# Channel-major attention output by small PE tiles, decay factors in PSUM and a second DMA transpose, in a fused recurrent-attention and MLP kernel

## The chip, the cores and the metric

The kernel runs on one core of a Trainium2 chip. The metric is device time in microseconds (us). Several runs of one program are compared by the mean of their fast runs; the profile is one of the runs. A run is called slow when it is over 1.5% above the fastest of the same kernel. The granted TensorE clock (the share of full speed that the matrix engine was given) does not tell such runs apart here: the changed kernel has slow runs at 0.935 and 0.901 and fast ones at 0.946 and 0.931. Medians are of all runs.

## The reference

Inputs have batch B=4, heads H=8, sequence S=768 and head size D=48. The attention is a recurrence over time, one 48x48 state per head. Its output is laid out as 3072 tokens x 384 channels and goes through an MLP with two gates of 1024 channels.

```python
for t in range(S):
    cur = einsum('bhd,bhe->bhde', u * k[t], v[t])
    y[t] = einsum('bhd,bhde->bhe', r[t], state + cur)
    state = w[t][..., None] * state + einsum('bhd,bhe->bhde', k[t], v[t])
x = y.transpose(0, 2, 1, 3).reshape(B * S, H * D)
out = maximum(x @ w1, x @ w2) @ w_out
```

## The kernel before

The sequence is cut into 12 units of 256 tokens of one batch entry. One partition holds two neighbouring tokens (index i). The engines are called PE (matrix products), DVE (VectorE), ACT (ScalarE), POOL or GpSimd, and SP, which here only issues DMAs. In each unit the kernel sums the logarithms of the decay, makes r' = r times the decay and k' = k over the decay, forms scores k'r', masks them, and multiplies by v. The state carried from earlier tokens enters through r'. The maximum of two gates is written as (w1 - w2)x, relu, plus w2 x, so wc = w2 w_out is precomputed. Every operation is a named token, and one list gives the order in which all of them are issued to the engines. All DMAs except the two cast weight loads are issued from one queue, that of SP, strictly in that order. The code is cut to the parts that the change touches.

```python
ORDER = """ ...
k.5 WL.4 Wt.4 evk.4 sc1.4 M1.4 xT.3 g0.3 g1.3 r0.3 r1.3 vd.4 yb.4 sc0.4 M0.4 iA.5 kp.5 ...
oc0.3 oa0.3 ob0.3 oc1.3 os0.3 tr.5 evr.5 kv.5 Sa.5 S1.5 Tf.5 row.5 lp.6 cs.6 AE.6 m.6 AO.6 z.6 ... """

def rp(n): nc.vector.tensor_mul(r_b[n % 2][:, :, :, 0:D], byi(U[n]["r"]), U[n]["A"])      # A in SBUF
def kp(n): nc.vector.tensor_mul(k_b[n % 2][:, :, :, 0:D], byi(U[n]["k"]), U[n]["iA"])     # iA in SBUF

def tr(n):      # r' turned on PE, 8 transposes; evr copies them out of PSUM on ACT
    ...
def evk(n):     # k' turned by the DMA
    nc.sync.dma_start_transpose(out=..., in_=k_b[n % 2].rearrange("s i h d -> s (i h d)"))
def S1(n):      # state cast on DVE, a zero block beside each head
    for e in range(2): nc.vector.tensor_copy(S_1[n % 2][q, :, e * D:(e + 1) * D], U[n]["Sa"][q])

def yb(n): ...  # y[token, channel] : 4 matmuls of 384 columns, then
def yi(n): ...  # 8 of 96 columns (incoming state) and
def ya(n): ...  # 32 of 48 columns (masked scores times v)
def x(n):  nc.scalar.copy(t, U[n]["y"][:, :, 0:HD])
def xT(n): nc.sync.dma_start_transpose(out=..., in_=U[n]["x"]...)   # y turned by the DMA for the MLP

def out_d(n, b):
    for i in range(2):
        nc.sync.dma_start(out=out[tok + i:tok + P:2, :], in_=U[n]["s", b][i * Q:(i + 1) * Q, :])
```

## Time and profile before

| what | value | from |
|---|---|---|
| time | 180.76 us median of 3 (180.09 to 180.93) | runs |
| span of the profile, granted clock | 178.3 us, 0.994 | page |
| busy PE / DVE / ACT / POOL | 135.8 / 126.7 / 91.7 / 106.8 us | page |
| first gate matmul, end of the last PE work | 44.66 us, 173.72 us | timeline of PE |
| gaps of PE in between, the rest | 7.7 us, 121.3 us | summed from that timeline |

From the first gate matmul on, every piece of time in which no matmul is under way is a gap, and what remains is PE work. "L389" and the like are lines of the kernel concerned, so one operation has different numbers in different kernels.

### The profile page before, as it was taken

The numbers are of one execution on the slowest core, as the hardware profiler recorded it, in microseconds if no ns is written. First come the engines' busy times: TensorE is split into PE (matmuls) and PEld (weight loads), VectorE is DVE, ScalarE is ACT, GpSimd is POOL, SyncE is SP. The second block draws the span as 40 slices with busy tenths as digits, with TensorE's granted clock in tenths as the row PEclk, the third lists the DMA queues.
The fourth block names the chain that finished last, engine by engine and source line by source line (L and its number), as shares of the span: only waits on it lengthen the run. The fifth ranks groups of instructions, "written<-read, shape, count | busy, mean of one in ns | idle before, by whom it ended". The sixth has DMA issues, their size and how long they took to land.

```text
span 178.3 us, 4629 instructions
## 1 busy us (share of the span) xinstructions
PE 135.8 (76%) x1912; PEld 87.9 (49%) x1912; DVE 126.7 (71%) x163; ACT 91.7 (51%) x153; POOL 106.8 (60%) x96
## 2 busy tenths in 40 slices
PE   0324064505999987978998889989999999999990
...
DMA  5988799699925979998889879999999988171513
GB/s 146 269 174 162 131 309 315 95 175 249 260 49 120 285 165 161 287 187 228 223 194 263 172 178 248 169 307 164 244 258 189 266 197 240 26 169 26 114 37 74
DMA packets 85445, 33.56 MB, mean 188 GB/s; under 512 B 80424, under 2 KB 84648, under 8 KB 85424
## 3 DMA queue, kind: packets, MB, share of 16 engines
...
## 4 chain that ended last, share of the span: by engine, by line
PE 33%; DMA 24%; DVE 17%; POOL 12%; issue 6%; SPq 4%; ACT 2%; POOLq 0%; ACTq 0%
PE go L456 11%; PE go L480 7%; DVE rn L263 6%; DMA wo_sb<-in_moe_w_out_dram 5%; POOL rku L299 5%; DVE S L360 4%; DMA w_sb<-in_moe_w_dram 4%; DMA xT<-x 4%; PE go L475 3%; DMA u_b<-in_u_dram 3%; DMA out_dram<-osb 3%; PE go L215 3%; DVE kn L267 3%; DMA lw<-in_w_dram 2%; DMA lr<-in_r_dram 2%
## 5 line engine op out<-in xcount | busy, mean ns | idle before, releaser
L456 PE MATMUL go<-xT,wd_sb 128*128 128x256 bf16 x288 | 37.4, 276 | 3.8 <-DMA xT<-x 1.9
L464 ACT ACTIVATE gT<-go 128x512 bf16<-128x512 f32 x48 | 28.5, 596 | 21.0 <-PE go L456 19.8
L393 DVE TENSOR_TENSOR M<-sc,mask 128x1024 bf16<-128x1024 f32 x24 | 29.3, 1219 | 12.8 <-PE sc L389 12.7
L480 PE MATMUL go<-wo_sb,gT 128*128 128x384 bf16 x192 | 35.3, 326 | 0.0
L294 POOL TENSOR_TENSOR rku<-lr,lk 128x768 f32<-128x768 f32 x12 | 21.8, 1814 | 20.2 <-issue 10.5
L456 PEld LDWEIGHTS <-wd_sb 128*128 128x128 bf16 x288 | 26.9, 99 | 10.5 <-issue 4.9
L299 POOL TENSOR_TENSOR rku<-rku,u_b 128x768 f32<-128x768 f32 x12 | 28.2, 2350 | 0.4 <-DMA u_b<-in_u_dram 0.3
L480 PEld LDWEIGHTS <-gT 128*128 128x128 bf16 x192 | 18.6, 98 | 14.1 <-issue 1.8
L263 DVE TENSOR_TENSOR rn<-lr,A 128x768 bf16<-128x768 f32 x12 | 25.1, 2095 | 0.1
L310 POOL TENSOR_TENSOR vd<-lv,dg 128x768 bf16<-128x768 f32 x12 | 17.7, 1475 | 11.2 <-DVE dg L305 10.7
L231 POOL TENSOR_TENSOR lp<-lw 128x384 f32<-128x384 f32 x12 | 17.4, 1447 | 3.1 <-ACT lw L226 3.1
L267 DVE TENSOR_TENSOR kn<-lk,iA 128x768 bf16<-128x768 f32 x12 | 18.6, 1550 | 0.1
L236 PE MATMUL ex<-lp,triS 128*128 128x384 f32 x24 | 13.0, 631 | 7.4 <-POOL lp L231 7.4
L360 DVE CAST S<-Sa 64x192 bf16<-64x192 f32 x24 | 17.6, 734 | 0.6
L485 ACT COPY osb<-go 128x384 f32<-128x384 f32 x24 | 11.3, 472 | 12.1 <-PE go L480 12.1
L389 PE MATMUL sc<-rT,kT 48*64 48x128 bf16 x384 | 10.7, 232 | 8.3 <-DMA kT<-kn 7.0
L326 ACT COPY rT<-tr 128x1024 bf16<-128x1024 bf16 x12 | 12.1, 1010 | 9.0 <-PE tr L319 9.0
L475 PE MATMUL go<-wc_sb,xT 128*128 128x384 bf16 x72 | 15.7, 328 | 0.0
L389 PEld LDWEIGHTS <-kT 48*64 48x64 bf16 x384 | 6.7, 112 | 17.0 <-DMA kT<-kn 8.9
L242 ACT ACTIVATE A<-ex 128x384 f32<-128x384 f32 x12 | 5.9, 490 | 15.5 <-PE ex L236 15.5
L305 DVE TENSOR_REDUCE dg<-rku 128x16 f32<-128x768 f32 x12 | 11.3, 942 | 3.4 <-POOL rku L299 3.4
L442 ACT CAST x<-y 128x768 bf16<-128x768 f32 x12 | 9.5, 791 | 7.9 <-PE y L433 7.8
...
## 6 DMA issues: line engine op xcount, KB each, us to landing
...
```

The source lines that it names most:

```text
L231: nc.gpsimd.tensor_add(t, U[n]["lw"][:, :, 0, :], U[n]["lw"][:, :, 1, :])
L263: nc.vector.tensor_mul(r_b[n % 2][:, :, :, 0:D], byi(U[n]["r"]), U[n]["A"])
L267: nc.vector.tensor_mul(k_b[n % 2][:, :, :, 0:D], byi(U[n]["k"]), U[n]["iA"])
L294: nc.gpsimd.tensor_mul(t, U[n]["r"], U[n]["k"])
L299: nc.gpsimd.tensor_mul(t, t, u_b.rearrange("p (h d) -> p h d", h=H).unsqueeze(1).to_broadcast([P, 2, H, D]))
L310: nc.gpsimd.tensor_mul(t.rearrange("p i h d -> p h i d"), U[n]["v"], U[n]["dg"].to_broadcast([P, H, 2, D]))
L360: nc.vector.tensor_copy(S_1[n % 2][q, :, e * D:(e + 1) * D], U[n]["Sa"][q])
L393: nc.vector.tensor_mul(t.rearrange("s e p t -> s (e p) t"), U[n]["sc", i].rearrange("s e p t -> s (e p) t"), mask[:, i].rearrange("s i q - ...
L456: nc.tensor.matmul(g[:, f, :], wd_sb[:, ko, fo * P:(fo + 1) * P], U[n]["xT"][:, :, ko, :], start=(f == 0 and ko == 0), stop=(f == 1 and ko ...
L464: nc.scalar.activation(U[n]["gT"][:, 2 * j:2 * j + 2].rearrange("p f j t -> p (f j t)"), U[n]["g", j].rearrange("p f j t -> p (f j t)"), A ...
L475: nc.tensor.matmul(t, U[n]["xT"][:, b, ko, :], wc_sb[:, ko, :], start=(ko == 0), stop=False)
L480: nc.tensor.matmul(U[n]["o", b], U[n]["gT"][:, fo, b, :], wo_sb[:, fo, :], start=False, stop=(fo == FO - 1))
```

## The change

It moves work off DVE and PE. The decay factors are computed in place in two PSUM banks. The attention output is produced with channels on the partitions, so it needs no transpose before the MLP. r' is then turned by the DMA, like k'. The state cast goes to ACT as one copy, and the whole order of issue is new, with the weights loaded first. The diff is shortened; its lines without code name what went.

```diff
-    ex, A, iA                               # sum in one PSUM bank, factors in SBUF
+    EX = ps.tile([P, 2, 512], F32, tag="ex", name="ex")      # sum and factors, one buffer, in place
-        nc.vector.tensor_mul(r_b[n % 2][:, :, :, 0:D], byi(U[n]["r"]), U[n]["A"])
+        nc.vector.tensor_mul(r_b[n % 2][:, :, :, 0:D], byi(U[n]["r"]), fac())
-    tr, evr, evk, x, xT(DMA)
+    def turn(n, name, src):
+        U[n][name] = t = wt_([P, 2, NP, P], BF16, name)
+        nc.sync.dma_start_transpose(out=..., in_=src[n % 2].rearrange("s i h d -> s (i h d)"))
+    OP["rT"] = lambda n: turn(n, "rT", r_b)
+    OP["kT"] = lambda n: turn(n, "kT", k_b)
-        for e in range(2): nc.vector.tensor_copy(S_1[...], U[n]["Sa"][q])
+        nc.scalar.copy(U[n]["S1"], U[n]["Sa"])
 ...
+    WIN = ((0, 0), (0, 1), (1, 1), (1, 2))      # head of the pair, 32-channel window
+    # 32 matmuls 48x32, 128 columns (incoming state), 64 matmuls 64x32, 128 columns (scores):
+    nc.tensor.matmul(out32(n, p, w, b), vwin(n, q, i, p, w * 32, 32), U[n]["M", i][q, WIN[w][0], p, :], ...)
+    def xT(n): nc.scalar.copy(t.rearrange("c b k t -> c b (k t)"), U[n]["y"][:, :, 0:HD])
 ...
+v.7 vb.7 vd.7 w.8 lw.8 lp.8 k.8 r.8 rk.8 rku.8 WL.6 out1.3 M0.6 sc1.6 rp.7 iA.7 rT.7 ... oc0.5 oa0.5
+ob0.5 oc1.5 os0.5 M1.6 ya.6 xT.6 out0.5 oa1.5 ob1.5 os1.5 kp.7 kT.7 kv.7 Sa.7 S1.7 cs.8 ... g0.6
+g1.6 r0.6 r1.6 ... yb.7 yi.7 sc0.7 M0.7 row.7 AE.8 g2.6 g3.6 r2.6 r3.6
```

More of the change, by code (lines that the diff above doesn't have):

```diff
@@ L17 @@
 ORDER = """
-w.0 k.0 lw.0 lp.0 cs.0 AE.0 m.0 r.0 u rk.0 rku.0 v.0 w.1 w2 k.1 vb.0 z.0 wt.0 AO.0 rp.0 tr.0
-iA.0 kp.0 kv.0 Sa.0 S1.0 lw.1 lp.1 cs.1 AE.1 m.1 AO.1 z.1 iA.1 dg.0 vd.0 kp.1 evk.0 evr.0 sc0.0
-M0.0 Tf.0 sc1.0 M1.0 yb.0 yi.0 ya.0 x.0 r.1 rp.1 tr.1 rk.1 evr.1 rku.1 dg.1 v.1 w.2 lw.2 vb.1
-kv.1 Sa.1 vd.1 S1.1 Tf.1 yb.1 lp.2 cs.2 AE.2 w1 wo wd.2 wd.0 wd.1 wcm.0 wce.0 xT.0 g0.0 r0.0
-row.0 m.2 AO.2 z.2 evk.1 sc1.1 M1.1 g1.0 r1.0 wt.1 wcm.1 wce.1 WL.0 Wt.0 dec.0 S0.0 wt.2 wcm.2
-wce.2 k.2 sc0.1 M0.1 iA.2 kp.2 g2.0 r2.0 g3.0 r3.0 yi.1 ya.1 x.1 r.2 v.2 rk.2 vb.2 w.3 lw.3 rp.2
@@ L24 @@
-rku.2 dg.2 oc0.0 oa0.0 ob0.0 oc1.0 os0.0 oa1.0 tr.2 evr.2 kv.2 Sa.2 S1.2 Tf.2 ob1.0 os1.0 row.2
-lp.3 cs.3 AE.3 k.3 WL.2 Wt.2 evk.2 sc1.2 M1.2 xT.1 g0.1 g1.1 r0.1 r1.1 row.1 m.3 AO.3 z.3 vd.2
-yb.2 sc0.2 M0.2 iA.3 kp.3 g2.1 r2.1 g3.1 r3.1 r.3 v.3 rk.3 vb.3 w.4 lw.4 rp.3 rku.3 dg.3 yi.2
-ya.2 x.2 WL.1 Wt.1 out0.0 oc0.1 oa0.1 ob0.1 oc1.1 os0.1 tr.3 evr.3 kv.3 Sa.3 S1.3 Tf.3 row.3
-lp.4 cs.4 AE.4 m.4 AO.4 z.4 oa1.1 ob1.1 os1.1 out1.0 k.4 WL.3 Wt.3 dec.1 evk.3 sc1.3 M1.3 xT.2
-g0.2 g1.2 r0.2 r1.2 vd.3 yb.3 sc0.3 M0.3 iA.4 kp.4 g2.2 r2.2 g3.2 r3.2 dec.2 S0.2 r.4 v.4 rk.4
@@ L30 @@
-vb.4 w.5 lw.5 rp.4 rku.4 dg.4 yi.3 ya.3 x.3 oc0.2 oa0.2 ob0.2 oc1.2 os0.2 tr.4 evr.4 kv.4 Sa.4
-S1.4 Tf.4 row.4 lp.5 cs.5 AE.5 m.5 AO.5 z.5 oa1.2 ob1.2 os1.2 out1.1 out0.1 k.5 WL.4 Wt.4 evk.4
-sc1.4 M1.4 xT.3 g0.3 g1.3 r0.3 r1.3 vd.4 yb.4 sc0.4 M0.4 iA.5 kp.5 g2.3 r2.3 g3.3 r3.3 dec.3
-S0.3 r.5 v.5 rk.5 vb.5 w.6 lw.6 rp.5 rku.5 dg.5 yi.4 ya.4 x.4 oc0.3 oa0.3 ob0.3 oc1.3 os0.3 tr.5
-evr.5 kv.5 Sa.5 S1.5 Tf.5 row.5 lp.6 cs.6 AE.6 m.6 AO.6 z.6 out0.2 oa1.3 ob1.3 os1.3 S0.1 out1.2
-k.6 WL.5 Wt.5 evk.5 sc1.5 M1.5 xT.4 g0.4 g1.4 r0.4 r1.4 vd.5 yb.5 sc0.5 M0.5 iA.6 kp.6 g2.4 r2.4
@@ L36 @@
-g3.4 r3.4 dec.4 S0.4 r.6 v.6 rk.6 vb.6 w.7 lw.7 rp.6 rku.6 dg.6 yi.5 ya.5 x.5 oc0.4 oa0.4 ob0.4
-oc1.4 os0.4 tr.6 evr.6 kv.6 Sa.6 S1.6 Tf.6 row.6 lp.7 cs.7 AE.7 m.7 AO.7 z.7 out0.3 oa1.4 ob1.4
-os1.4 out1.3 k.7 WL.6 Wt.6 evk.6 sc1.6 M1.6 xT.5 g0.5 g1.5 r0.5 r1.5 vd.6 yb.6 sc0.6 M0.6 iA.7
-kp.7 g2.5 r2.5 g3.5 r3.5 dec.5 S0.5 r.7 v.7 rk.7 vb.7 w.8 lw.8 rp.7 rku.7 dg.7 yi.6 ya.6 x.6
-oc0.5 oa0.5 ob0.5 oc1.5 os0.5 tr.7 evr.7 kv.7 Sa.7 S1.7 Tf.7 row.7 lp.8 cs.8 AE.8 m.8 AO.8 z.8
-out0.4 oa1.5 ob1.5 os1.5 out1.4 k.8 WL.7 Wt.7 evk.7 sc1.7 M1.7 xT.6 g0.6 g1.6 r0.6 r1.6 vd.7
@@ L42 @@
-yb.7 sc0.7 M0.7 iA.8 kp.8 g2.6 r2.6 g3.6 r3.6 dec.6 S0.6 r.8 v.8 rk.8 vb.8 w.9 lw.9 rp.8 rku.8
-dg.8 yi.7 ya.7 x.7 oc0.6 oa0.6 ob0.6 oc1.6 os0.6 tr.8 evr.8 kv.8 Sa.8 S1.8 lp.9 cs.9 AE.9 m.9
-AO.9 z.9 out0.5 oa1.6 ob1.6 os1.6 out1.5 k.9 evk.8 sc1.8 M1.8 xT.7 g0.7 g1.7 r0.7 r1.7 vd.8 yb.8
-sc0.8 M0.8 iA.9 kp.9 g2.7 r2.7 g3.7 r3.7 dec.7 S0.7 r.9 v.9 rk.9 vb.9 w.10 lw.10 rp.9 rku.9 dg.9
-yi.8 ya.8 x.8 oc0.7 oa0.7 ob0.7 oc1.7 os0.7 tr.9 evr.9 kv.9 Sa.9 S1.9 lp.10 cs.10 AE.10 m.10
-AO.10 z.10 out0.6 oa1.7 ob1.7 os1.7 out1.6 k.10 evk.9 sc1.9 M1.9 xT.8 g0.8 g1.8 r0.8 r1.8 vd.9
@@ L48 @@
-yb.9 sc0.9 M0.9 iA.10 kp.10 g2.8 r2.8 g3.8 r3.8 r.10 v.10 rk.10 vb.10 w.11 lw.11 rp.10 rku.10
-dg.10 yi.9 ya.9 x.9 oc0.8 oa0.8 ob0.8 oc1.8 os0.8 tr.10 evr.10 kv.10 Sa.10 S1.10 lp.11 cs.11
-AE.11 m.11 AO.11 z.11 out0.7 oa1.8 ob1.8 os1.8 out1.7 k.11 evk.10 sc1.10 M1.10 xT.9 g0.9 g1.9
-r0.9 r1.9 vd.10 yb.10 sc0.10 M0.10 iA.11 kp.11 g2.9 r2.9 g3.9 r3.9 r.11 v.11 rk.11 vb.11 rp.11
-rku.11 dg.11 yi.10 ya.10 x.10 oc0.9 oa0.9 ob0.9 oc1.9 os0.9 tr.11 evr.11 kv.11 Sa.11 S1.11
-out0.8 oa1.9 ob1.9 os1.9 out1.8 evk.11 sc1.11 M1.11 xT.10 g0.10 g1.10 r0.10 r1.10 vd.11 yb.11
@@ L54 @@
-sc0.11 M0.11 g2.10 r2.10 g3.10 r3.10 yi.11 ya.11 x.11 oc0.10 oa0.10 ob0.10 oc1.10 os0.10 out0.9
-oa1.10 ob1.10 os1.10 out1.9 xT.11 g0.11 g1.11 r0.11 r1.11 g2.11 r2.11 g3.11 r3.11 oc0.11 oa0.11
-ob0.11 oc1.11 os0.11 out0.10 oa1.11 ob1.11 os1.11 out1.10 out0.11 out1.11
+w.0 w1 lw.0 w2 wt.2 wd.2 k.0 r.0 u v.0 lp.0 cs.0 wo wcm.2 wd.1 m.0 z.0 AO.0 w.1 row.0 wd.0 AE.0
+rp.0 rT.0 iA.0 rk.0 rku.0 dg.0 vd.0 vb.0 lw.1 lp.1 kp.0 kv.0 kT.0 cs.1 Sa.0 S1.0 Tf.0 m.1 z.1
+AO.1 AE.1 yb.0 yi.0 sc1.0 M1.0 sc0.0 wce.2 M0.0 ya.0 k.1 r.1 rp.1 rk.1 rku.1 dg.1 iA.1 kp.1 wt.1
@@ new lines @@
+wcm.1 wce.1 wt.0 wcm.0 wce.0 v.1 vb.1 vd.1 w.2 lw.2 lp.2 k.2 r.2 rk.2 rku.2 xT.0 kv.1 Sa.1 S1.1
+Tf.1 g0.0 g1.0 r0.0 r1.0 cs.2 m.2 z.2 AO.2 AE.2 rT.1 kT.1 yb.1 yi.1 sc0.1 M0.1 row.1 dg.2 g2.0
+r2.0 g3.0 r3.0 WL.0 Wt.0 v.2 vb.2 vd.2 w.3 k.3 lw.3 lp.3 r.3 rk.3 rku.3 sc1.1 WL.1 rp.2 iA.2
+rT.2 row.2 oc0.0 oa0.0 ob0.0 os0.0 out0.0 oc1.0 oa1.0 M1.1 ya.1 xT.1 ob1.0 os1.0 kp.2 kT.2 kv.2
+Sa.2 S1.2 Tf.2 cs.3 m.3 z.3 AO.3 g0.1 r0.1 g1.1 r1.1 yb.2 yi.2 sc0.2 AE.3 WL.2 g2.1 g3.1 r2.1
+r3.1 dg.3 out1.0 M0.2 sc1.2 v.3 vb.3 vd.3 w.4 k.4 lw.4 lp.4 r.4 rk.4 rku.4 row.3 rp.3 iA.3 rT.3
@@ new lines @@
+oc0.1 oa0.1 ob0.1 oc1.1 os0.1 out0.1 M1.2 ya.2 xT.2 oa1.1 ob1.1 os1.1 kp.3 kT.3 kv.3 Sa.3 S1.3
+Tf.3 cs.4 g0.2 g1.2 r0.2 r1.2 WL.3 m.4 z.4 AO.4 AE.4 dec.0 S0.0 yb.3 yi.3 sc0.3 g2.2 g3.2 r2.2
+r3.2 dg.4 M0.3 sc1.3 v.4 vd.4 vb.4 w.5 k.5 lw.5 lp.5 r.5 rk.5 rku.5 Wt.1 rp.4 iA.4 rT.4 row.4
+oc0.2 oa0.2 ob0.2 oc1.2 os0.2 out0.2 M1.3 ya.3 xT.3 dec.1 S0.1 oa1.2 ob1.2 os1.2 out1.1 kp.4
+kT.4 kv.4 Sa.4 S1.4 Tf.4 cs.5 m.5 z.5 AO.5 dg.5 g0.3 g1.3 r0.3 r1.3 WL.4 AE.5 yb.4 yi.4 sc0.4
+M0.4 g2.3 g3.3 r2.3 r3.3 v.5 vb.5 vd.5 w.6 lw.6 lp.6 k.6 r.6 rk.6 rku.6 sc1.4 row.5 rp.5 iA.5
@@ new lines @@
+rT.5 oc0.3 oa0.3 ob0.3 oc1.3 os0.3 out0.3 Wt.2 dec.2 S0.2 WL.5 M1.4 ya.4 xT.4 oa1.3 ob1.3 os1.3
+out1.2 kp.5 kT.5 kv.5 Sa.5 S1.5 Tf.5 cs.6 m.6 z.6 AO.6 g0.4 g1.4 r0.4 r1.4 yb.5 yi.5 sc0.5 AE.6
+dg.6 g2.4 g3.4 r2.4 r3.4 M0.5 sc1.5 v.6 vb.6 vd.6 w.7 lw.7 lp.7 k.7 r.7 rk.7 rku.7 rp.6 iA.6
+rT.6 oc0.4 oa0.4 ob0.4 os0.4 oc1.4 out0.4 M1.5 ya.5 xT.5 oa1.4 ob1.4 os1.4 kp.6 kT.6 kv.6 Sa.6
+S1.6 Tf.6 cs.7 m.7 z.7 AO.7 dg.7 Wt.3 dec.3 S0.3 g0.5 g1.5 r0.5 r1.5 yb.6 yi.6 sc0.6 row.6 AE.7
+g2.5 g3.5 r2.5 r3.5 v.7 vb.7 vd.7 w.8 lw.8 lp.8 k.8 r.8 rk.8 rku.8 WL.6 out1.3 M0.6 sc1.6 rp.7
@@ new lines @@
+iA.7 rT.7 Wt.5 Wt.4 dec.4 S0.4 out1.4 oc0.5 oa0.5 ob0.5 oc1.5 os0.5 M1.6 ya.6 xT.6 out0.5 oa1.5
+ob1.5 os1.5 kp.7 kT.7 kv.7 Sa.7 S1.7 cs.8 Tf.7 m.8 z.8 AO.8 dg.8 g0.6 g1.6 r0.6 r1.6 dec.5 S0.5
+yb.7 yi.7 sc0.7 M0.7 row.7 AE.8 g2.6 g3.6 r2.6 r3.6 v.8 vb.8 vd.8 w.9 lw.9 lp.9 k.9 r.9 rk.9
+rku.9 sc1.7 WL.7 Wt.6 dec.6 S0.6 rp.8 iA.8 rT.8 oc0.6 oa0.6 ob0.6 oc1.6 os0.6 out0.6 M1.7 ya.7
+xT.7 oa1.6 ob1.6 os1.6 kp.8 kT.8 kv.8 Sa.8 S1.8 cs.9 m.9 z.9 AO.9 dg.9 g0.7 g1.7 r0.7 r1.7 yb.8
+yi.8 sc0.8 AE.9 g2.7 g3.7 r2.7 r3.7 M0.8 sc1.8 out1.5 v.9 vb.9 vd.9 w.10 lw.10 lp.10 k.10 r.10
@@ new lines @@
+rk.10 rku.10 rp.9 iA.9 rT.9 oc0.7 oa0.7 ob0.7 os0.7 oc1.7 out0.7 M1.8 ya.8 xT.8 out1.6 oa1.7
+ob1.7 os1.7 kp.9 kT.9 kv.9 Sa.9 S1.9 cs.10 m.10 z.10 AO.10 g0.8 g1.8 r0.8 r1.8 yb.9 yi.9 sc0.9
+AE.10 g2.8 g3.8 r2.8 r3.8 dg.10 M0.9 sc1.9 v.10 vb.10 vd.10 w.11 lw.11 lp.11 k.11 r.11 rk.11
+rku.11 v.11 vb.11 rp.10 iA.10 rT.10 oc0.8 oa0.8 ob0.8 oc1.8 os0.8 out0.8 M1.9 ya.9 xT.9 oa1.8
+ob1.8 os1.8 kp.10 kT.10 kv.10 Sa.10 S1.10 cs.11 m.11 z.11 AO.11 g0.9 g1.9 r0.9 r1.9 out1.8 dg.11
+vd.11 Wt.7 dec.7 S0.7 yb.10 yi.10 sc0.10 AE.11 g2.9 g3.9 r2.9 r3.9 M0.10 sc1.10 rp.11 iA.11
@@ L57 @@
+rT.11 oc0.9 oa0.9 ob0.9 oc1.9 os0.9 M1.10 ya.10 xT.10 oa1.9 ob1.9 os1.9 kp.11 kT.11 kv.11 Sa.11
+S1.11 g0.10 g1.10 r0.10 r1.10 yb.11 yi.11 sc0.11 out0.9 g2.10 g3.10 r2.10 r3.10 M0.11 sc1.11
+oc0.10 oa0.10 ob0.10 oc1.10 out1.7 os0.10 out0.10 out1.9 M1.11 ya.11 xT.11 oa1.10 ob1.10 os1.10
+g0.11 r0.11 g1.11 r1.11 g2.11 g3.11 r2.11 oc0.11 oa0.11 r3.11 ob0.11 oc1.11 os0.11 out0.11
+oa1.11 ob1.11 os1.11 out1.10 out1.11
 """
@@ L91, in _body @@
     DP = 64
+    VW = 80
     NU = NC * B
@@ L124, in _body @@
     mask = const.tile([P, 2, 2, Q], F32)
-    sel = const.tile([P, 2, 2, Q], BF16)
     MZ = [const.tile([P, 2, H, DP], F32, name=f"mz{i}") for i in range(2)]
@@ L132, in _body @@
             nc.vector.memset(t.rearrange("p i h d -> p (i h) d")[:, :, D:DP], 0.0)
-    S_f = [const.tile([P, NP, D], F32, name=f"Sf{b}") for b in range(B)]
-    T_f = [const.tile([P, NP, D], F32, name=f"Tf{b}") for b in range(B)]
-    S_0 = [const.tile([P, NP, 2 * D], BF16, name=f"S0{b}") for b in range(B)]
-    S_1 = [const.tile([P, NP, 2 * D], BF16, name=f"S1{b}") for b in range(2)]
-    nc.vector.memset(sel, 0.0)
+    v_b = [const.tile([P, 2, H, VW], BF16, name=f"vn{i}") for i in range(3)]
+    for t in v_b:
+        nc.gpsimd.memset(t[:, :, ::2, D:VW], 0.0)
+    S_f = [const.tile([P, NP, DP], F32, name=f"Sf{b}") for b in range(B)]
+    T_f = [const.tile([P, NP, DP], F32, name=f"Tf{b}") for b in range(B)]
+    S_0 = [const.tile([P, NP, DP], BF16, name=f"S0{b}") for b in range(B)]
+    EX = ps.tile([P, 2, 512], F32, tag="ex", name="ex")
     for b in range(2):
@@ L142, in _body @@
         for i in range(2):
-            nc.vector.tensor_copy(sel[q, i, i, :], ident[q, q])
             for i2 in range(2):
@@ L146, in _body @@
                                       (triI if (i, i2) == (0, 1) else triS)[q, q])
-    for t in S_f + S_1 + S_0:
+    for t in S_f + S_0:
         nc.vector.memset(t, 0.0)
@@ L234, in cs, with ex3, fac, m @@
     def cs(n):
-        U[n]["ex"] = t = pt_([P, H, D], F32, "ex")
-        nc.tensor.matmul(t.rearrange("p h d -> p (h d)"), triS,
-                         U[n]["lp"].rearrange("p h d -> p (h d)"))
+        nc.tensor.matmul(EX[:, 0, 0:HD], triS, U[n]["lp"].rearrange("p h d -> p (h d)"))
+    def ex3():
+        return EX[:, 0, 0:HD].rearrange("p (h d) -> p h d", h=H)
+    def fac():
+        return EX[:, :, 0:HD].rearrange("p i (h d) -> p i h d", h=H)
+    @op
+    def m(n):
+        nc.vector.tensor_add(MZ[n % 2][:, 0, :, 0:D], ex3(), U[n]["lw"][:, :, 0, :])
+    @op
+    def z(n):
+        nc.vector.tensor_add(MZ[n % 2][:, 1, :, 0:D], ex3(), U[n]["lp"])
+    @op
+    def AO(n):
+        nc.scalar.activation(fac()[:, 1], MZ[n % 2][:, 0, :, 0:D], AF.Exp)
     @op
     def AE(n):
-        U[n]["A"] = t = wt_([P, 2, H, D], F32, "A")
-        nc.scalar.activation(t[:, 0], U[n]["ex"], AF.Exp)
-    @op
-    def m(n):
-        nc.vector.tensor_add(MZ[n % 2][:, 0, :, 0:D], U[n]["ex"], U[n]["lw"][:, :, 0, :])
-    @op
-    def z(n):
-        nc.vector.tensor_add(MZ[n % 2][:, 1, :, 0:D], U[n]["ex"], U[n]["lp"])
-    @op
-    def AO(n):
-        nc.scalar.activation(U[n]["A"][:, 1], MZ[n % 2][:, 0, :, 0:D], AF.Exp)
+        nc.scalar.activation(ex3(), ex3(), AF.Exp)
     @op
     def iA(n):
-        U[n]["iA"] = t = wt_([P, 2, H, D], F32, "iA", 1)
-        nc.scalar.activation(t, MZ[n % 2][:, :, :, 0:D], AF.Exp, scale=-1.0)
+        nc.scalar.activation(fac(), MZ[n % 2][:, :, :, 0:D], AF.Exp, scale=-1.0)
     @op
     def rp(n):
-        nc.vector.tensor_mul(r_b[n % 2][:, :, :, 0:D], byi(U[n]["r"]), U[n]["A"])
+        nc.vector.tensor_mul(r_b[n % 2][:, :, :, 0:D], byi(U[n]["r"]), fac())
     @op
     def kp(n):
-        nc.vector.tensor_mul(k_b[n % 2][:, :, :, 0:D], byi(U[n]["k"]), U[n]["iA"])
+        nc.vector.tensor_mul(k_b[n % 2][:, :, :, 0:D], byi(U[n]["k"]), fac())
     @op
@@ L287, in vb @@
     def vb(n):
-        U[n]["vb"] = t = wt_([P, H, 2, D], BF16, "vb", 3)
-        nc.gpsimd.tensor_copy(t, U[n]["v"])
+        nc.gpsimd.tensor_copy(v_b[n % 3][:, :, :, 0:D], byi(U[n]["v"]))
     @op
@@ L311, in vd @@
                              U[n]["dg"].to_broadcast([P, H, 2, D]))
-    @op
-    def tr(n):
-        U[n]["tr"] = tp = pt_([P, NP, 2, 2, Q], BF16, "tr")
-        for i in range(2):
-            for p in range(NP):
-                nc.tensor.transpose(
-                    tp[:, p, :, i, :],
-                    r_b[n % 2][:, i, 2 * p:2 * p + 2, :].rearrange("s r d -> s (r d)"), ident)
-    @op
-    def evr(n):
-        U[n]["rT"] = t = wt_([P, NP, 2, 2, Q], BF16, "rT")
-        nc.scalar.copy(t, U[n]["tr"])
-    @op
-    def evk(n):
-        U[n]["kT"] = t = wt_([P, 2, NP, P], BF16, "kT")
+    def turn(n, name, src):
+        U[n][name] = t = wt_([P, 2, NP, P], BF16, name)
         nc.sync.dma_start_transpose(out=t.rearrange("d i p q -> d (i p) q"),
-                                    in_=k_b[n % 2].rearrange("s i h d -> s (i h d)"))
+                                    in_=src[n % 2].rearrange("s i h d -> s (i h d)"))
+    OP["rT"] = lambda n: turn(n, "rT", r_b)
+    OP["kT"] = lambda n: turn(n, "kT", k_b)
     @op
```

93 lines of the change are left out of this document (49 added, 44 removed).

## The prediction

> **What bounds the kernel now.** I read the page first, then the chain in order of time, the groups by shape, single lines with the spread of their durations, then the loading of the weights in the timeline of the first 50 us, and the DMA queue's own instructions.
>
> From the page of the kernel before (engine totals, then two rows of the 40 slices of 4.46 us, each digit a tenth busy):
>
> ```profile
> PE 135.8 (76%) x1912; PEld 87.9 (49%) x1912; DVE 126.7 (71%) x163; ACT 91.7 (51%) x153; POOL 106.8 (60%) x96
> PE   0324064505999987978998889989999999999990
> DMA  5988799699925979998889879999999988171513
> ```
>
> PE is busy 0 to 6 tenths in the first ten slices (44.6 us) and 7 to 9 in nearly all later ones. So there are two stages: a start of 44.7 us, in which the weights arrive and attention unit 0 is made, and 128.8 us in which PE works through twelve units (first gate matmul at 44.66 us, last PE work at 173.5). A tail of 4.8 us follows (copy and store of the last rows).
>
> From the chain that ended last, in order of time (start us, us, what), most of one unit:
>
> ```profile
> 139.00 0.81 PE go L456 x6
> 139.81 0.43 PE y L409 x4
> 140.25 0.35 PE sc L389 x16
> 140.60 1.42 PE go L456 x12
> 142.01 0.34 PE y L421 x8
> 142.35 0.51 PE y L433 x32
> 142.86 0.59 PE go L475 x3
> 143.45 1.30 PE go L480 x8
> 144.75 0.49 PE go L475 x3
> 145.24 0.04 issue
> 145.28 0.62 PE tr L319 x8
> 145.90 0.38 PE y L344 x16
> ```
>
> The reader sees the price of each PE step without gaps. One unit: gates 2.9 (24 in 2.93 at the end of the chain), second layer 16 in 2.6, wc product 0.59+0.49, L409 0.43, scores 2 x 0.35, L421 0.34, L433 0.51, transposes 0.62, k'v 0.4, prefix sum 0.9. Sum 10.5 us. The starts of the L409 group in the timeline (59.63 to 160.29 us, nine units) give 11.2 us per unit: 12.2 and 12.1 at first, about 11.1 in the middle, 10.7 to 9.9 at the end. So about 0.7 us of each unit is PE waiting. In the chain these waits are DVE work: r' 2.5 us, k' 1 to 1.3, the state cast 1.3.
>
> From the groups by line (busy us, mean ns; then idle time before):
>
> ```profile
> L263 DVE TENSOR_TENSOR rn<-lr,A 128x768 bf16<-128x768 f32 x12 | 25.1, 2095 | 0.1
> L267 DVE TENSOR_TENSOR kn<-lk,iA 128x768 bf16<-128x768 f32 x12 | 18.6, 1550 | 0.1
> L360 DVE CAST S<-Sa 64x192 bf16<-64x192 f32 x24 | 17.6, 734 | 0.6
> L393 DVE TENSOR_TENSOR M<-sc,mask 128x1024 bf16<-128x1024 f32 x24 | 29.3, 1219 | 12.8 <-PE sc L389 12.7
> ```
>
> Per unit DVE has 2.1 + 1.55 + 2 x 0.73 + 2 x 1.22, and reduce 0.94, two sums 1.1, Sa and Tf 0.7: 10.3 us, as much as PE. The views of single lines (min/median/max ns) tell why the first three are dear:
>
> ```profile
> L263 DVE TENSOR_TENSOR rn<-lr,A x12: 946/2561/2569, 9.6 to 154.7; 128x768 bf16<-128x768 f32 x12
> L393 DVE TENSOR_TENSOR M<-sc,mask x24: 1211/1223/1226, 23.2 to 161.2; 128x1024 bf16<-128x1024 f32 x24
> ```
>
> The same product takes 946 ns or 2,569 ns, while the mask product, with one operand in PSUM, is always 1.21 to 1.23 us.
>
> **What the Trainium skill says.** (1) "SBUF — State Buffer", section Who interferes with whom: a DVE instruction with two SBUF inputs contends with GpSimd reads, and so does a two-port copy or cast; one with at most one SBUF input does not. The trace agrees: r' spreads over 946 to 2,569 ns, the mask product over 15. (2) "TensorEngine Tiling (Array Packing)", Performance Considerations and Restrictions: tiling speeds up TensorE but not PSUM evacuation; column tiling excludes fast weight loads, and different row tiles must not use the same PSUM bank together. The kernel before shows 64-column tiles working at 22 ns a pair; no run yet shows 32-column ones. (3) "TensorE: Matmul & The Clock Gate", Part 3, The mechanism: a weight load overlaps running matmuls only where the row group differs. The trace fits: k'v takes 0.37 us for 32 pairs when its row tile alternates, but 0.38 us for 16 pairs in the last chunk, where it does not (12 against 24 ns).
>
> **The change, part by part.**
>
> *Factors in PSUM.* r' and k' now read one operand from PSUM. I put both at the uncontended 0.95 us: DVE saves 1.15 + 0.6 = 1.75 us per unit, and GpSimd is blocked less (its u product is 1.81 us alone, 2.35 on average). The cost is a serial chain through one buffer: sum 0.9, m and z 1.1, two exponentials 1.0, r' 0.95, inverse 0.84, k' 0.95, some 5.7 us plus handovers. It fits in an 11 us unit.
>
> *State casts.* Two DVE casts (1.47 us) become one 128x256 ACT copy, about 0.4 us by the 0.47 us of the 128x384 copy. GpSimd's two 0.34 us casts become one. DVE falls to some 10.3 - 1.75 - 1.47 + 0.1 = 7.2 us per unit. DVE stops being a bound.
>
> *r' by the DMA.* PE loses 0.62 us (tr) and ACT the 1.01 us copy. The transpose of x disappears, as the output is already channel-major; ACT still copies y (0.79 us). DMA trades 6 blocks for 8 of 128x128. At the end of the trace one pair of transposes (458 KB) holds the DMA share at 0.98 for about 2.5 us, so the trade costs about 0.35 us of DMA. With four loads (at 325 GB/s, seen in windows, 4.8 us), stores 1.8 and both transposes, 9.2 us per unit: below 11. The wait for xT (4.1 us and 2.6 us in two places of the chain) goes; r' and k' each get a DMA wait of 3.5 us, which the new order covers with PE work.
>
> *Channel-major output.* L409 4 x 384 columns (0.43 us) becomes 12 pairs of 64 columns: at L433's 16 ns, 0.2. L421 and L433 (0.85 us, 8 + 32 pairs) become 32 + 64 pairs with 128 moving columns. Scores, also 128 columns in 64-row tiles, take 22 ns a pair. The 64 of L433 alternate row tiles; with twice the column tiles but one column tile visited twice running, I take 18 ns: 1.15 us. The 32 of L421 go two by two on a row tile; 26 ns, between 22 and 24 with a margin: 0.83 us. Together 2.0, so +1.15. PE per unit: 10.5 - 0.62 - 0.23 + 1.15 = **10.8 us**. PE work does not fall; what can fall is its waiting, from 0.7 to an estimated 0.2 us: 11.0 us a unit.
>
> *The start.* Before, w_out is issued only at 32.4 us (behind GpSimd's work of unit 1) and lands at 42.1. Now w1, w2 and w_out go first. w2 took 6.95 us alone; with w and w1 beside it I estimate landing at 14 us, w_out at 22. But k, r, v of unit 0 are issued behind the w2 transpose, so at 15 to 17 us, landing 19 to 22. Then: GpSimd products to 24, reduce to 25, k' to 26, its transpose to 31, scores and masks one after the other to 35, output 36, two weight products and k'v of unit 1 to 40.5. I put the first gate at **40.5 us**, against 44.7, with all three weight products done by then (before, two were still to come, 2.6 us).
>
> *Sum.* From the first gate: 12 x 6.6 us of MLP + 11 x 4.2 of attention = 125.4, less 1.2 for first-chunk units without the incoming state, plus 11 x 0.2 of waits = 126.4. 40.5 + 126.4 + 4.8 = 171.7 us of span; the timed median is 2.5 us over the span (180.76 against 178.3): 174.2, which I round up to **174.5 us**, as the estimates of the start leave out handovers.
>
> **The rivals.** *Small tiles cost more than thought.* If 32-column pairs take 40 ns, L421 and L433 become 3.8 us, PE 12.7 us per unit, and the time some 195 us. For it: without row alternation a pair doubled to 24 ns, and the skill page says fast weight loads are off. Against it: scores already run in column tiles at 22 ns. *The waits vanish and tiles are quick.* At 13 ns a pair PE needs 10.1 us per unit: 166 us. *A transpose arrives late.* k' is transposed behind stores in the queue; DMA_TRANSPOSE takes 1.25 us to issue and 3.2 to 5.1 to land. Half a microsecond per unit gives 180 us. *The start does not shorten* (units' loads behind weights): 178 to 180 us.
>
> **Range and chances.** The start is uncertain by 3 us, PE per unit by 0.4 (5 us in all). Range 167 to 181 us. Faster by over 2% (under 177.1) 0.70; within 2% 0.22; slower 0.08.
>
> **What would show it.** Right: r' and k' at 0.95 us with hardly any spread; DVE busy near 90 us in all; L421 and L433 successors summing to 2 us per unit; first gate near 40 us; w_out landed before 25; units 11 us apart with PE at 9 tenths. Wrong: PE waiting on rT or kT transposes in the middle; a pair cost of 30 ns or more; a first gate at 44 us or later; ACT waits for the prefix sum showing the single factor buffer as the bound.

## The result

The changed kernel is slower: 190.6 us median of four runs (188.34 to 193.59), against 180.84 us for the kernel before in the same rounds. The ratio is 1.040, 95% interval 1.027 to 1.054. A ratio here is the mean time of one kernel's fast runs over the mean of the other's in the same rounds, so it is not quite the ratio of the medians. Two of the four runs count as slow (192.7 and 193.6 us). The profiled run is a fast one, 188.51 us, span 186.6, clock 0.946. The prediction of 174.5 us, range 167 to 181, was wrong.

From the page of the changed kernel: totals, then PE and its granted clock in 40 slices of 4.67 us.

```profile
PE 135.2 (72%) x2536; PEld 85.9 (46%) x2536; DVE 90.8 (49%) x132; ACT 83.3 (45%) x153; POOL 94.1 (50%) x91
PE   0303227777969969829949989699996497999980
PEclk9999999999996999965996999969999999999996
```

DVE fell from 126.7 to 90.8 us of work, as intended. But PE's row, which was 8 to 9 in the middle before, has holes of 2, 4 and 6, and behind some of them the granted clock falls to 6 and 5 tenths.

| from the timeline of PE | before | changed | difference |
|---|---|---|---|
| first gate matmul at | 44.66 | 40.12 | -4.5 |
| gaps of PE after it | 7.7 | 19.7 | +12.0 |
| PE work after it | 121.3 | 121.3 | 0.0 |
| from PE's end to the end of the span | 4.6 | 5.5 | +0.9 |
| span | 178.3 | 186.6 | +8.3 |

So the start was gained as predicted, and twelve microseconds of waiting were added. The waits of the changed kernel (who waited for what: us in total, times, longest) say what for:

```profile
PE sc L379 <- DMA kT<-kn: 17.8, 9, 3.9
ACT lw L227 <- DMA lw<-in_w_dram: 16.8, 8, 3.2
```

Scores wait for the transposed k' in nine of the twelve units, 17.8 of the 19.7 us. After its first gate the kernel before waited 0.93 us for the same thing. The chain that ended last (start us, us, what) and the DMA queue's own instructions in the timeline show one such wait, of unit 5:

```profile
93.66 0.47 DVE mz L250
94.15 3.13 DMA kT<-kn
97.28 0.04 issue
97.32 0.42 PE sc L379 x16
97.74 2.38 PE go L456 x12
```

```profile
88.06 0.95 DVE L270 TENSOR_TENSOR kn<-lk,ex 128x768 bf16<-128x768 f32 x1 [0.26 <-ACT ex L262]
...
90.85 2.01 SPq L281 DMA_DIRECT2D WL<-row  x1
92.91 1.14 SPq L491 DMA_DIRECT2D out_dram<-osb  x2
94.15 1.28 SPq L318 DMA_TRANSPOSE kT<-kn  x1
```

k' was complete at 89.01. Its transpose was issued at 94.15, 5.1 us later, because SP first waited 0.6 us for what the stores needed and then issued four stores and a small reload. The data landed 3.1 us after the issue. Over units 1 to 11 this lag from DVE's end to the issue is 2.0 us on average, and from issue to landing it is 3.1 to 5.0 us in the nine waits. In units 2 to 11 of the kernel before the lag was 0.4 us (unit 1, 9.3 us, belongs to its start).

The last line of the chain above also shows the second loss. Twelve gate matmuls take 2.38 us, where a full clock gives 1.42. A wait of 1.64 us before 55.90 us is followed by this (the view by windows: stretch and its length, busy us and instructions of PE, PEld, DVE, ACT, POOL, then granted clock, DMA share, GB/s):

```profile
55.00:56.00 1.00, 0.10 (x8) 0.10 (x12) 0.42 (x1) 0.47 (x2) 0.00 (x0) 1.00 0.62 71
57.00:58.00 1.00, 1.00 (x7) 0.58 (x5) 1.00 (x2) 0.60 (x1) 0.00 (x0) 0.53 0.56 104
59.00:60.00 1.00, 1.00 (x4) 0.46 (x3) 1.00 (x1) 0.00 (x0) 0.00 (x0) 0.50 1.16 323
61.00:62.00 1.00, 1.00 (x13) 0.43 (x14) 0.00 (x0) 0.71 (x1) 1.00 (x2) 1.00 1.13 297
```

The clock is halved from about 57.1 to 60.5 us and then restored. PE work stayed at 121.3 us although the new matmuls cost less; e5 below puts that down to the clock.

The halvings do not follow from the length of a single gap. They begin at 57.05, 80.95, 98.01 and 121.91 us, whole multiples of 3.41 us apart. Here are two stretches of that grid in which the clock held, and the one before the first halving:

```profile
39.99:43.40 3.41, 2.77 (x61) 1.83 (x45) 1.87 (x4) 1.50 (x3) 2.63 (x3) 1.00 0.92 164
43.40:46.82 3.42, 2.69 (x48) 2.00 (x49) 2.22 (x3) 2.26 (x5) 1.94 (x2) 1.00 0.99 251
53.64:57.05 3.41, 1.77 (x45) 1.33 (x45) 1.63 (x2) 1.83 (x4) 0.79 (x1) 1.00 0.80 148
```

The stretches before the four halvings have PE busy for 1.77, 1.17, 0.95 and 1.42 us. No other full stretch at full clock between the first gate and 180 us has under 1.79. A gap of 1.37 us before 44.13 falls across two stretches and left the clock alone. The limit is not exact: in e6 a stretch with 1.68 us was not followed by a halving. This is read from traces; no experiment moved a gap for it.

### The profile page after: what moved, and what is told of

Read it like the earlier page. It is cut to its first block, busy times and chain, and to the rows that moved or that the text cites. A ratio compares the mean times of both kernels' runs of the same rounds, so it can differ in the third digit from the quotient of the medians.

```text
span 186.6 us, 5852 instructions
## 1 busy us (share of the span) xinstructions
PE 135.2 (72%) x2536; PEld 85.9 (46%) x2536; DVE 90.8 (49%) x132; ACT 83.3 (45%) x153; POOL 94.1 (50%) x91
## 4 chain that ended last, share of the span: by engine, by line
PE 38%; DMA 34%; SPq 9%; POOL 6%; DVE 4%; ACT 4%; issue 3%; POOLq 0%; DVEq 0%; ACTq 0%
DMA kT<-kn 14%; PE go L480 13%; PE go L456 11%; DMA lw<-in_w_dram 9%; PE go L475 6%; DMA lr<-in_r_dram 6%; DMA w_sb<-in_moe_w_dram 5%; PE sc L379 4%; SPq L208 3%; SPq L178 3%; PE y L440 2%; SPq L491 2%; POOL rku L301 2%; POOL rku L296 2%; PE y L333 2%
## 5 line engine op out<-in xcount | busy, mean ns | idle before, releaser
L456 PE MATMUL go<-xT,wd_sb 128*128 128x256 bf16 x288 | 39.6, 292 | 0.1
L296 POOL TENSOR_TENSOR rku<-lr,lk 128x768 f32<-128x768 f32 x12 | 21.7, 1810 | 24.8 <-DMA lr<-in_r_dram 24.8
L456 PEld LDWEIGHTS <-wd_sb 128*128 128x128 bf16 x288 | 28.9, 104 | 9.1 <-issue 2.4
L291 POOL CAST vn<-lv 128x768 bf16<-128x768 f32 x12 | 9.9, 825 | 31.8 <-DMA lv<-in_v_dram 26.1
L379 PE MATMUL sc<-rT,kT 48*64 48x128 bf16 x384 | 11.6, 248 | 19.2 <-DMA kT<-kn 17.8
L301 POOL TENSOR_TENSOR rku<-rku,u_b 128x768 f32<-128x768 f32 x12 | 21.7, 1810 | 0.9
L227 ACT ACTIVATE lw<-lw 128x768 f32<-128x768 f32 x12 | 10.1, 842 | 16.9 <-DMA lw<-in_w_dram 16.8
L270 DVE TENSOR_TENSOR kn<-lk,ex 128x768 bf16<-128x768 f32 x12 | 11.4, 952 | 12.2 <-ACT ex L262 12.2
L475 PE MATMUL go<-wc_sb,xT 128*128 128x384 bf16 x72 | 17.1, 351 | 0.0
L254 ACT ACTIVATE ex<-mz 128x384 f32<-128x384 f32 x12 | 5.9, 494 | 22.5 <-DVE mz L250 21.2
L349 DVE TENSOR_TENSOR Sa<-y,Sf 128x256 f32<-128x256 f32 x12 | 5.1, 424 | 21.9 <-PE y L333 19.2
L232 POOL TENSOR_TENSOR lp<-lw 128x384 f32<-128x384 f32 x12 | 12.0, 998 | 2.8 <-ACT lw L227 2.8
L262 ACT ACTIVATE ex<-mz 128x768 f32<-128x768 f32 x12 | 9.6, 802 | 7.6 <-DVE rn L266 7.5
```

Of the source, the lines that this page charges most:

```text
L232: nc.gpsimd.tensor_add(t, U[n]["lw"][:, :, 0, :], U[n]["lw"][:, :, 1, :])
L296: nc.gpsimd.tensor_mul(t, U[n]["r"], U[n]["k"])
L301: nc.gpsimd.tensor_mul(t, t, u_b.rearrange("p (h d) -> p h d", h=H).unsqueeze(1).to_broadcast([P, 2, H, D]))
L379: nc.tensor.matmul(sc[q, e, p, :], kT[d, i, p, q], rT[d, :, p, q])
L456: nc.tensor.matmul(g[:, f, :], wd_sb[:, ko, fo * P:(fo + 1) * P], U[n]["xT"][:, :, ko, :], start=(f == 0 and ko == 0), stop=(f == 1 and ko ...
L475: nc.tensor.matmul(t, U[n]["xT"][:, b, ko, :], wc_sb[:, ko, :], start=(ko == 0), stop=False)
```

## The experiments

Theory A: the order and occupancy of the one DMA queue delay the transposes and the loads. Theory B: the data itself is too much, that is r' beside k' makes transposes land late. A third candidate, the granted clock, was watched in every run. All runs gave correct results. Each group of four was run on one chip with its own runs of the kernel before (medians 180.12, 180.94 and 180.74 us). Gaps and work are those of the profiled run; a star marks a profile that fell in the slow state. The clock is the mean of the whole span. In e3, e4 and e10 its records begin early and hold a halved stretch of 13.7 us before the first gate (in e10 up to 0.9 us after it); in most others they begin only near the gate. So the figures of these three do not compare with the rest. How far SP's queue is occupied, given below in per cent, is taken from the rows of its timeline from 40 to 150 us; short gaps between issues of one kind count as occupied.

| run | median us | ratio to before (95%) | gaps | PE work | clock |
|---|---|---|---|---|---|
| changed kernel | 190.6 | 1.040 (1.027 to 1.054) | 19.7 | 121.3 | 0.946 |
| e1 loads early* | 191.7 | 1.057 (1.046 to 1.069) | 21.8 | 125.5 | 0.927 |
| e2 stores late | 189.6 | 1.044 (1.030 to 1.057) | 20.1 | 119.3 | 0.971 |
| e3 both | 183.1 | 1.016 (1.008 to 1.025) | 14.9 | 121.4 | 0.913 |
| e4 r' by PE | 181.2 | 1.006 (0.997 to 1.014) | 11.7 | 123.1 | 0.926 |
| e5 stores by ACT | 175.8 | 0.967 (0.957 to 0.976) | 12.2 | 116.7 | 0.985 |
| e6 stores by ACT, loads early | 177.5 | 0.979 (0.971 to 0.988) | 13.9 | 116.1 | 0.990 |
| e7 r' by PE, e1 and e2* | 175.1 | none: one fast run | 5.4 | 121.4 | 0.980 |
| e8 r' by PE, e6* | 176.8 | 0.968 (0.956 to 0.980) | 8.8 | 122.9 | 0.966 |
| e9 as e7, WL late | 174.7 | 0.964 (0.959 to 0.969) | 5.8 | 119.8 | 0.983 |
| e10 kernel before, stores by ACT | 186.6 | 1.034 (1.030 to 1.038) | 13.3 | 120.7 | 0.954 |
| e11 stores by ACT, w early | 173.6 | 0.960 (0.956 to 0.965) | 9.9 | 116.3 | 0.983 |
| e12 as e11, r' by PE, WL late | 172.8 | 0.959 (0.955 to 0.963) | 5.5 | 120.1 | 0.983 |

### e1: loads one unit earlier

```diff
-    for name in ORDER.split():
+    for name in early(ORDER.split()):     # at the place of w.n, k.n, r.n, v.n from unit 3 (v: 2) on: load n + 1
```

> The changed kernel with the loads of w, k, r and v moved one unit earlier in the DMA queue's order, nothing else. Theory A (order of the one DMA queue: k' is transposed late because its trigger waits behind stores, and ACT and GpSimd wait for loads issued just before use): the waits of ACT and GpSimd for loads (17, 25 and 26 us in all) nearly vanish, but the wait of PE for the k' transpose stays at over 10 us of its 17.8; 183 to 187 us. Theory B (the DMA engines or the landing of transposes are overloaded by r' beside k'): within 2 us of the changed kernel, 188 us.

No gain: 191.7 us. The waits for w fell from 16.8 to 8.1 us and those of GpSimd for v from 26.1 to 3.2. But PE still waited 17.6 us for k', and the lag of its transpose grew from 2.0 to 3.0 us. Both theories' numbers were missed (183 to 187 and 188 us), theory A's by more. Late loads were real, yet taking part of them away gained nothing. This profile is of a slow run (194.3 us), so its times are rough.

### e2: stores behind the transpose

```diff
+    for name in late(ORDER.split()):      # every out token moved behind the next kT token
```

> The changed kernel with every store of the output moved behind the next k' transpose in the queue's order, nothing else. Theory A: the lag from the end of k' on DVE to the issue of its transpose falls from 2.0 us on average to under 0.7, the wait of PE for it from 17.8 to under 9 us, the granted clock rises to 0.97 or more, 178 to 183 us. Theory B: the lag falls, but landing takes over 4.5 us instead, the wait stays over 14 us; 186 to 189 us.

Half of this came true: the lag fell to 0.5 us and the wait for k' to 5.7 us. The time did not follow, 189.6 us. From the waits of this run:

```profile
ACT lw L242 <- DMA lw<-in_w_dram: 32.4, 12, 4.4
PE y L348 <- ACT xT L463: 12.6, 8, 2.2
PE sc L394 <- DMA kT<-kn: 5.7, 5, 1.5
```

With the stores in front of them, the loads of w came later still, by which ACT lost 32 us. In ACT's order the copy of y stands behind the logarithm that waited, and PE waited 12.6 us for that copy; e11 tests this. The total gap stayed at 20 us: the wait had only changed its name.

### e3: both orders

> Both edits of the queue's order together. Theory A: waits for the k' transpose under 5 us, clock 0.98 or more, 170 to 177 us, so faster than the kernel before. Theory B: 185 to 189 us.

183.1 us, half-way. Neither theory's number was met. Gaps are 14.9 us and the lag of k' is 1.9 us again, with r' at 2.3. Its edit is those of e1 and e2 together. In the stretch from 40 to 150 us SP's queue spends 92% of the time issuing (88% in the changed kernel, 83% before; by single instructions 90%, 87% and 81%). These two orders together did not make room in it.

### e4: r' by PE again

```diff
-    OP["rT"] = lambda n: turn(n, "rT", r_b)
+    def tr(n):   # 8 PE transposes into the bank of the scores, in front of kv.n
+    def evr(n):  nc.scalar.copy(t, U[n]["tr"])
```

> The changed kernel with r' turned by PE and copied by ACT again (as in the kernel before, in the bank of the scores), the order otherwise unchanged: one part undone. Theory A: the stores stay ahead of k', so the wait for the k' transpose stays over 10 us, PE has 0.6 us more per unit; 183 to 189 us. Theory B: without r' on the DMA the k' transpose lands in time, wait under 6 us, 176 to 181 us.

181.2 us, level with the kernel before. One part undone gave back the whole loss. That lies nearest to theory B's number, but the wait for k' was still 9.7 us, which B had put under 6, and the lag 1.25 us. The run alone does not separate the theories, because taking r' off the DMA takes its bytes and its issue time away together: SP's queue is 75% occupied here instead of 88%. e5 does separate them.

### e5: the stores from ACT's queue

```diff
-            nc.sync.dma_start(out=out[tok + i:tok + P:2, :],
+            nc.scalar.dma_start(out=out[tok + i:tok + P:2, :],
```

> The changed kernel with the 48 output stores issued from ACT's queue instead of the one that issues everything else; order and bytes unchanged. Theory A (triggers wait in one in-order queue: the stores take 41 us of its issue time and wait for ACT's copies): lag from k' to its transpose under 0.7 us, PE's wait for k' under 9 us, 180 to 184 us; late loads stay. Theory B (the data in flight, 8 blocks of r' more than before beside the loads, makes the transposes land late): bytes are the same, so landing stays 3.1 to 5.0 us and the time 187 to 190 us.

175.8 us, 3.3% faster than the kernel before, by one word in the source, and better than theory A had said. Transfers, bytes and order of tokens are those of the changed kernel; only the issuer of 48 stores differs. SP's queue is 72% occupied, the lag of k' 0.6 us. From the waits of this run:

```profile
PE y L333 <- ACT xT L448: 7.5, 9, 2.5
PE sc L379 <- DMA kT<-kn: 2.8, 3, 1.3
```

This rules out theory B as the main cause, since all bytes of r' are still there (it had said 187 to 190 us). In the three waits for k' landing still took 4.7 to 5.0 us, so it was not faster landing that helped, but earlier issue. The move takes two things out of SP's order at once: the stores' issue time (29.6 us by single instructions; the 41 us of the expectation count the gaps between two of them) and their waits for ACT's copies (13.3 us of SP's own waiting in the changed kernel). No run tells these two apart. PE executes exactly the matmuls of the changed kernel and spends 116.7 instead of 121.3 us on them, at a clock of 0.985 instead of 0.946. I put those 4.6 us down to the lower clock: after the first gate it is halved for 17.1 us in the changed kernel and for 3.4 us in e5. Together with 7.5 us fewer gaps they make up the 12.2 us between the spans (186.6 and 174.4).

### e6 and e8: the same with all loads early

e6 has the edits of e5 and e1, e8 those and r' by PE.

> Stores from ACT's queue and the loads one unit earlier. Theory A: neither stores nor late loads are left in the way; lags of r' and k' under 1 us, waits of ACT and GpSimd for loads under 10 us in all, 172 to 179 us. Theory B: no better than with the loads early alone (190 us).

> r' by PE, stores from ACT's queue, loads one unit earlier: the least work in the queue that holds the k' transpose. Theory A: the fastest of all, lag of k' near 0 in every unit, PE waits under 5 us, clock 0.97 or more, 168 to 175 us. Theory B: 180 to 183 us.

The times are 177.5 and 176.8 us. The first lies in theory A's range, but its lags (1.3 us on average for r' and for k') and its waits for loads (9.1 us of ACT, 24.8 of GpSimd, half of that in the start) do not; the second missed. Neither gained over e5. My shift put two sets of loads at one place. In e6 SP issued six loads from 43.7 to 51.2 us, WL to 53.6, and only then the transpose of r' of unit 2, ready since 47.7. The burst was an error in my edit; that it cost the gain is read from the trace and not tested alone.

### e7 and e9: everything in the one queue, with r' by PE

e7 has the edits of e1, e2 and e4. e9 also holds WL, the reload of the decay row, behind kT.

> r' by PE (which alone gave 181.2) with both order edits (which alone gave 183.1). Theory A (the queue's occupancy is what counts, and each of these takes some of it): they add up, PE waits under 6 us after the first gate, 172 to 178 us. Theory B (only the bytes of r' counted): 180 to 183 us, as with r' by PE alone.

> r' by PE, loads early, and stores and the small reload of the decay row (WL) behind the k' transpose, all in the one queue. What is left of the lags there (1.9, 3.4 and 1.4 us in three units) stood behind WL's wait for its row. Theory A: these lags go, PE waits for k' under 2 us, 169 to 174 us and steadier than with the stores alone (175.1). If the granted clock rather than the queue decides by now: 174 to 177 us.

Medians of 175.1 and 174.7 us. e7 had one fast run of four (171.45 us, clock 0.999), so it has no interval. In e7 the lags left were 1.9, 3.4 and 1.4 us in three units. In e9 none was over 1.0, and its six runs spread over 3.3 us instead of 5.6. But e9 missed theory A's range (169 to 174 us) and its wait for k' was 2.7 us, not under 2; its time lies in the range given for the case that the clock decides (174 to 177). Without any help of ACT's queue, the order and one transfer less per unit are therefore enough to beat the kernel before.

### e10: the kernel before with its stores from ACT

The edit of e5, in the kernel before.

> Control: the kernel before with its stores issued from ACT's queue, nothing else. Theory A says the move helps the changed kernel because its k' and r' transposes stand behind stores in a tight place; the kernel before waits only 2.8 us for its two transposes after the first gate and is bound by DVE and PE, so 178 to 182 us, at most 1% either way. If the queue had been the bound before as well: 172 to 176 us.

A miss in the other direction: 186.6 us, 3.4% slower. SP's queue is then only 52% occupied and it gains nothing. From the waits of the kernel before and of this run:

```profile
PE go L456 <- ACT osb L485: 1.7, 3, 0.7
```

```profile
PE go L456 <- ACT osb L485: 7.1, 8, 1.4
```

The waits of PE for this copy grew by 5.4 us, the gaps in all by 5.6. In the kernel before the gates need the PSUM bank that ACT empties just then, and in ACT's order store triggers stand around this copy. Two of them took 1.12 us in the timeline, at 104.2. Issuing is not free for the engine that does it; it only suits a kernel whose order leaves it room.

### e11 and e12: the version that beats both

e11 is e5 with the load of w alone one unit early. e12 adds r' by PE and WL behind kT.

> Stores from ACT's queue (175.8) with the load of w alone one unit earlier. Left over there were 7.5 us in which PE waits for ACT's copy of y, as ACT stands in order behind the logarithm that waits for w (13 us). Theory A: those waits fall under 3 us without the burst of double loads that all four early loads caused, 171 to 174 us. Rival (ACT is held by its own store issues): no gain, 175 to 178 us.

> r' by PE, stores from ACT's queue, w one unit early, WL behind the k' transpose: all that was found in the way taken out. Theory A: lags of k' near 0, PE waits under 5 us in all after the first gate, clock over 0.98, 168 to 173 us. PE work alone from the first gate is about 12 x 10.3 = 124 us, so 40 + 124 + 5 + 2 = 171 us is the floor of this form. If the clock decides: 173 to 177 us.

173.6 and 172.8 us, so 4% faster than the kernel before. In e11 the wait of PE for the copy of y fell from 7.5 to 2.8 us, as theory A said. In e12 the gaps were 5.5 us, a little over the 5 that it had said. In e12 no transpose of k' waits for its issue any more; the same place as shown for the changed kernel, in the timeline:

```profile
82.62 0.95 DVE L308 TENSOR_TENSOR kn<-lk,ex 128x768 bf16<-128x768 f32 x1 [0.42 <-ACT ex L300]
...
83.66 1.48 SPq L356 DMA_TRANSPOSE kT<-kn  x1
85.26 0.67 SPq L319 DMA_DIRECT2D WL<-row  x1
```

k' ends at 83.57 and is issued 0.09 us later, the longest lag of units 1 to 11 in this run. WL stands behind it, where it harms nobody. The intervals of e11 and e12 overlap, so whether PE or the DMA should turn r' is not decided: e12 has 4.4 us fewer gaps and 3.8 us more PE work. All six runs of e12 were fast.

## Why the prediction was wrong

**The start was right.** 40.5 us was predicted for the first gate, 40.12 measured, and the steps in between came within about 1.5 us of their places (reduce done at 24.2 for 25, k' at 25.1 for 26, first scores at 29.9 for 31, second masks done at 33.8 for 35). w2 landed at 11.9 us instead of 14, and w_out before 17.0 instead of 22.

**DVE was right.** I had put r' and k' at 0.95 us and DVE's work near 90 us. The views of single lines of the changed kernel (min/median/max ns), against 946 to 2,569 (r') and 948 to 2,746 (k') before:

```profile
L266 DVE TENSOR_TENSOR rn<-lr,ex x12: 943/944/953, 19.5 to 160.2; 128x768 bf16<-128x768 f32 x12
L270 DVE TENSOR_TENSOR kn<-lk,ex x12: 944/954/955, 24.2 to 162.2; 128x768 bf16<-128x768 f32 x12
```

With one operand in PSUM the spread is gone. The u product on GpSimd also ran at 1.81 us each time instead of 2.35 on average.

**The small tiles were mis-sized, in the change's favour.** I gave L421's and L433's successors 2.0 us per unit, at 26 and 18 ns a pair. The chain shows them at full clock:

```profile
152.22 0.62 PE y L440 x53
...
163.19 0.24 PE y L419 x16
163.43 0.60 PE y L440 x52
```

From unit 4 on L419 has 32 pairs in a unit, in two groups of 16, and L440 has 64 (the chain counts only part of them). The first group of 16 stands before the scores and also takes 0.24 us (e5, 100.65 to 100.89). That is 2 x 0.24 + 0.60 = 1.08 us: 15 and 9.4 ns a pair. By the same prices a unit of PE work is 10.5 - 0.62 (transposes) - 0.15 (L401's 0.28 for 0.43) + 0.23 (1.08 for 0.85) = 10.0 us, not the 10.8 that I had. So of the rival "The waits vanish and tiles are quick" (13 ns a pair, 166 us) the second half came true and the first did not.

**The step that failed** is "r' and k' each get a DMA wait of 3.5 us, which the new order covers with PE work", and with it the term "11 x 0.2 of waits" of the sum. The gaps were 19.7 us, not 2.2. I had read the landing and not the queue: the lag from the end of k' to the issue of its transpose, 2.0 us on average, was missing. I had checked that bytes fit (9.2 of 11 us) but not that issue times fit. The issues of the kernel before (loads at 0.5 to 1.2 us, four stores at 2.4, two transposes at 1.3 each) already filled 83% of SP's queue. The rival "A transpose arrives late" was the right mechanism; I gave it 0.5 us per unit and 180 us. It took 1.5 us per unit (17.8 over 12). Slower by over 2% had been given a chance of 0.08.

**One step was absent.** No part of the sum had the granted clock in it. It fell behind the gaps, and comparison with e5 puts that at 4.6 us. By the same rows, full-clock work in the changed kernel would be some 115 us (12 x 6.6 of MLP, ten units of 2.4 of attention, nearly as much of unit 1, ten prefix sums of 0.9), an estimate; so e5's 116.7 still holds a part of the loss, about half of the 3.4 us in which its clock was halved.

The miss adds up: span 186.6 against 171.7 predicted is 14.9 us. Gaps give +17.5 (19.7 for 2.2), PE work -2.9 (121.3 for 124.2), the tail +0.7 and the start -0.4. That PE work came so near is luck: by the estimate above the cheaper matmuls took off some 9 us, and the lower clock put some 6 back.

**What stays open:** how much one more gap costs, as that hangs on where it falls in the 3.41 us stretches; how much of the gain in e5 is the stores' issue time and how much their waits; and whether PE or the DMA should turn r'.

## What to carry to other kernels

Treat a DMA queue that one engine issues like an engine: add up its issue times per period and see which waits stand in front of an urgent transfer, before judging by bytes or by landing time. When a wait is removed by reordering a full queue, look for the next waiter (e2 took 12 us from one wait and added as much to others); here, taking issues out of the queue gave the gain. The issuer that takes them over must have room in its own order: the same edit gave 7% in one kernel (0.967 for 1.040 of the kernel before) and cost 3.4% in the other.

## What the Trainium skill lacked or had wrong

- "DMA: Bandwidth & Descriptors", Rules for kernel authors, says that spreading DMAs over SP, ACT and GpSimd does not help bandwidth and only saves the sequencer's issue time. It does not say how much that can be, nor what it costs the engine that takes the issues over. Here the changed kernel took 175.8 us with the stores issued by ACT, against 190.6 with all transfers by SP, and the kernel before took 186.6 against 180.7. The page has no issue times measured on trn2 (only cycle counts of "previous generations" beside trn3's). In the changed kernel an issue lasted 0.4 to 2.8 us for a load, 0.5 to 1.7 for a store and 1.23 to 3.3 for a transpose of 128x1024.
- "TensorE: Matmul & The Clock Gate", Part 1, says the start-to-start of matmuls never drops below about 25 ns however small N is. With 64x32 tiles 64 pairs with 128 columns added 0.60 us to the chain, 9.4 ns each; its Part 3, on tiles, is closer with about 4 ns between starts.
- The same page, Part 1, gives an idle window of about 3.4 us before the clock is halved. No idle window was needed here: in the changed kernel a stretch of 3.41 us with PE busy for 1.77 was followed by 3.4 us at a clock of 0.50, and its longest gap was 1.64 us.
- "TensorEngine Tiling (Array Packing)", Restrictions and Gotchas, says that column tiling excludes fast weight loads. It names no cost; the pairs with 32 columns took 15 and 9.4 ns each, less than the 22 ns of the 64-column scores.
